# Block-sparse attention and a gated FFN on one core: FFN groups of one chunk in place of two, another order of the attention-value matmuls, and a new order list

## The chip, the cores and the metric

The kernel runs on one core of one Trainium2 chip. Times are device microseconds of that core. The tensor engine is called PE, the vector engine DVE, the scalar engine ACT, GpSimd POOL and the sync engine, which here only issues DMAs, SP.

## The reference, cut to what matters

```python
# q, k, v: (4 batches, 8 heads, 768 tokens, 64); blocks of 32 tokens
scores = np.matmul(q, k.transpose(0, 1, 3, 2)) / np.sqrt(64)
mask   = |block_i - block_j| <= 1, or first/last block row or column, or one of 3 sampled blocks
attn   = softmax(np.where(mask, scores, -1e9))
x      = np.matmul(attn, v)          # heads side by side: (3072 tokens, 512)
gate   = 1 / (1 + np.exp(-(x @ w_gate)))     # 512 -> 1536
val    = x @ w_val
out    = (gate * val) @ w_out                # 1536 -> 512, float32
```

## The kernel before, in words

The work is cut into 12 **chunks** of 256 tokens (three for each batch) and, within a chunk, four **pairs** of heads: 48 pairs, numbered 0 to 47 in the order of the loops over chunk and head pair.

For each pair, `attend` issues three score tiles (`scores`, line 640), each with 256 of the 768 keys against the chunk's 256 queries for both heads. The 64-row matmuls of the two heads use the two halves of the PE array at the same time. ACT takes the exponential of each tile out of PSUM (line 658, tile `pt`), DVE multiplies it by the 0/1 mask (line 666). Then `values` (line 681) forms 24 matmuls of 65 columns into one PSUM bank: 2 query blocks (`jq`) x 2 heads (`hd`) x 6 key blocks (`j`). The 65th column of the values is one, so that it gives the sum of the weights. DVE takes the reciprocal of that sum (line 691) and multiplies (line 695). The result is turned to lie with features on partitions: for the first three chunks by PE (line 720) and a DVE copy (line 725), for the others by a DMA transpose that SP issues (line 708). It is written into a tile `x0` to `x3`.

The FFN (`ffn`) takes the chunks in **groups**. For each of 12 blocks of 128 hidden features, PE forms gate and value projections (line 746), each four matmuls of the group's width; ACT takes tanh of the half gate (line 767, tile `tg`), DVE forms (tanh + 1) x value (line 774, tile `h`). Each **gate step** in the list below is one of the two projections of a block. Output projections (line 791) sum over the 12 blocks for 128 tokens at a time into one bank, in **output steps** of two matmuls; DVE or ACT halves the sum (lines 805, 809) and SP stores it (line 814). In the kernel before, the groups are

```python
GROUPS = [[0], [1], [2], [3, 4], [5, 6], [7, 8], [9, 10], [11]]
```

so that four of them are 512 tokens wide, where a gate matmul has 512 columns and gate and value take a bank each, and four are 256 wide, where both share a bank.

The order of all instructions is made when the program is built. Each step is recorded with an engine, a duration, its inputs and outputs, and a priority (`Plan.op`); `Plan.run` then lays the steps out in time with those durations (an exponential is put at 0.915 us, a value set at 0.79), gives out PSUM banks and ring buffers, and writes each engine's instructions down in the order found. On the chip, each engine runs its own list in order and waits only on semaphores. Where the planner has a choice, it takes the lowest priority number, disturbed by random numbers from `SEED`. From pair `CHAIN` = 28 on, the order of PE's steps is fixed by hand as a chain of **rounds**, one per pair, spelled by

```python
ROUND = "SoVgggoo"
```

in which S is the three score tiles of pair m, V the values of pair m - 1, g about two units of gate steps (a 512-wide step is two units), and o an output step. `WANT` and `READY` hold back outputs and gates until their inputs can be there. `FETCH` says after which pair's scores the later loads of q, k and v are placed, `CAST_LATE` shifts the priority of their casts and transposes. Rings: q, k and v have two staging buffers each, `pt` has 12, each `x` tile has 3.

At the start, PE runs dummy matmuls (line 380) where it would wait, and POOL loads the first batch in half precision, then the FFN weights (lines 521, 531).

Of the kernel before, what the change touches and what calls it, by code (L numbers as in the profile page):

```python
# [9 lines left out]
f16 = mybir.dt.float16  # L10
f32 = mybir.dt.float32
# [7 lines left out]
NJ = S // 128  # L19
NP = H // 2  # L20
NCH = 3
CH = 256
DM = H * D
DFF = 1536
NF = DFF // 128
# [2 lines left out]
VW = 96  # L28
SPIN = 22.0
NMASK = 1  # L30
SEED, MIX = 43, 0.4
WANT, READY = 4, 1
Q0P, M1P, M2P = -39.2, 14, 17
XR, HR, HOLD, HN = 3, 2, 0.4, 1
EARLY = [(0, 0), (1, 0), (0, 1), (0, 2), (0, 3)]
FETCH = ((6, 1), (3, 2))
CHAIN, GLAG, OLAG, ROUND = 28, 9, 16, "SoVgggoo"
EDGES = [0, 768, 1536]
LAND = dict(sbi=1.7, mi=1.6, ident=3.2, e0=3.4, e1=3.3, q=3.1, kb=4.4, k=3.5)
FIRST = [  # L40
# [1 line left out]
]  # L42
HALF = [(0, 0), (0, 1), (0, 2), (0, 3)]
TURN_PE = 3
CAST_LATE = 20
GROUPS = [[0], [1], [2], [3, 4], [5, 6], [7, 8], [9, 10], [11]]
WIDE = CH * max(len(ns) for ns in GROUPS)


class Buf:  # L50
# [220 lines left out]
def kernel(  # L271
# [32 lines left out]

    P = Plan()
    for name, n in (
        ("qs", 2), ("ks", 2), ("vs", 2), ("q16", 4), ("k16", 4), ("qT", 8), ("kT", 8),
        ("v16", 8), ("vh", 4), ("pt", 12), ("rz", 2), ("x16", 4), ("tg", 2), ("y", 3),
    ):
        P.ring(name, n)  # L310
    P.banks(8)
# [284 lines left out]
    def build_mask(c, prio, behind):  # L596
# [21 lines left out]

    group_of = {n: (g, i) for g, ns in enumerate(GROUPS) for i, n in enumerate(ns)}
    xT = {  # L620
        (g, p): sb(f"x{p}", [128, WIDE], f16) for g in range(len(GROUPS)) for p in range(NP)
    }

    valued, scored = {}, []
# [1 line left out]
    def attend(n, p, seq):  # L626
        b, c = divmod(n, NCH)
        masked = n < NMASK
        pts = []
        for tt in range(NCH):  # L630
            st, pt = psb([2, 512], homes=PAIR, span=2), sb("pt", [128, 2, 2, CH], f16)

            def scores(tt=tt, st=st):
                qT, kT = tr["q", b, p](), tr["k", b, p]()
                for jj in range(2):
                    for own in (0, 1) if masked else (1,):
                        for hd in range(2):
                            r = slice(hd * 64, hd * 64 + 64)
                            l, m = (kT, qT) if own else (e24(), bias())
                            nc.tensor.matmul(  # L640
                                st()[:, hd, jj * CH : (jj + 1) * CH],
                                l[r, 2 * tt + jj, :],
                                m[r, 2 * c : 2 * c + 2, :],
                                start=not (own and masked), stop=bool(own),
                            )

            need = [tr["q", b, p], tr["k", b, p]]
            o = P.op(
                "PE", 0.43 if masked else 0.215, scores, reads=[*need, e24, bias] if masked else need,
                writes=[st], prio=seq, mode="row", behind=scored[-1:],  # L650
            )
            if (n, p, tt) == (0, 0, 0):
                o.deps.remove(late)
            scored.append(o)
            o.paired, o.twin = (n, p) not in EARLY and 4 * n + p < CHAIN, psb([2, 512], homes=PAIR, span=2)
            P.op(
                "ACT", 0.915,
                lambda st=st, pt=pt: nc.scalar.activation(  # L658
                    pt().rearrange("p h j q -> p h (j q)"), st(), AF.Exp, scale=SCALE
                ),  # L660
                reads=[st], writes=[pt], prio=seq,
            )

            def masks(tt=tt, pt=pt):
                t = pt().rearrange("p h j q -> p h (j q)")
                nc.vector.tensor_tensor(  # L666
                    t, t, mask()[:, c, tt].unsqueeze(1).to_broadcast([128, 2, 512]), op=ALU.mult
                )

            if not masked:  # L670
                P.op("DVE", 0.61, masks, reads=[pt], writes=[pt], after=[mask_ops[c, tt]], prio=seq)
            pts.append(pt)

        o, rz, x16 = psb([4, 128]), sb("rz", [128, 4, 1], f32), sb("x16", [128, 2, 128], f16)

        def values():
            v_ = v16[b, p]()
            for jq in range(2):
                for hd in range(2):
                    for j in range(NJ):  # L680
                        nc.tensor.matmul(  # L681
                            o()[:, 2 * jq + hd, 0:65],
                            pts[j // 2]()[:, hd, j % 2, jq * 128 : jq * 128 + 128],
                            v_[:, hd, j, 0:65],
                            start=(j == 0), stop=(j == NJ - 1),
                        )

        valued[n, p] = P.op("PE", 0.79, values, reads=[*pts, v16[b, p]], writes=[o], prio=seq + (3.05 if n == 0 and p < 3 else 0.1), mode="full")
        hold = HOLD if n < HN else 0.0
        P.op(  # L690
            "DVE", 0.2, lambda: nc.vector.reciprocal(rz(), o()[:, :, 64:65]), reads=[o], writes=[rz], prio=seq - 5  # L691
        ).hold = hold
        P.op(
            "DVE", 0.36,
            lambda: nc.vector.tensor_tensor(  # L695
                x16().rearrange("p j (h d) -> p (j h) d", d=64),
                o()[:, :, 0:64],
                rz().to_broadcast([128, 4, 64]),
                op=ALU.mult,
            ),  # L700
            reads=[o, rz], writes=[x16], prio=seq - 5,
        ).hold = hold
        g, i = group_of[n]
        dst = xT[g, p]
        if n >= TURN_PE:
            P.op(
                "SP", 1.2,
                lambda: nc.sync.dma_start_transpose(
                    dst()[:, i * CH : (i + 1) * CH].rearrange("p (j q) -> p j q", j=2),
                    x16().rearrange("p j m -> p (j m)"),  # L710
                ),
                reads=[x16], writes=[dst], prio=seq - 5, dma=0.45,
            )
            return
        tT = psb([2, 128], f16)

        def turn():
            dst()
            for jq in range(2):
                nc.tensor.transpose(tT()[:, jq, :], x16()[:, jq, :], ident16())  # L720

        P.op("PE", 0.12, turn, reads=[x16, ident16], writes=[tT, dst], prio=seq - 5, mode="full").hold = hold
        P.op(
            "DVE", 0.28,
            lambda: nc.vector.tensor_copy(
                dst()[:, i * CH : (i + 1) * CH], tT().rearrange("p j q -> p (j q)")
            ),
            reads=[tT], writes=[dst], prio=seq - 5,
        ).hold = hold


    hts, gates, outs, ends = {}, [], [], []

    def ffn(g, seq):
        w = CH * len(GROUPS[g])
# [2 lines left out]
        first = seq - 90 if last else seq  # L738
        for f in range(NF):
            both = psb([512])  # L740
            pair = [(both, 0), (both, 256) if w == 256 else (psb([512]), 0)]
            for k, ((t, z), (nm, wt)) in enumerate(zip(pair, (("g", wg), ("v", wv)))):

                def go(t=t, z=z, wt=wt, f=f):
# [13 lines left out]
                        behind=gates[-1:],  # L758
                    )
                )  # L760
                gates[-1].units, gates[-1].group = w // 256, g
                gates[-1].ready = 4 * GROUPS[g][-1] + 4 + READY
            tg, h_ = sb("tg", [128, WIDE], f32), sb(f"h{f}", [128, WIDE], f16)
            hts[g, f] = h_
            P.op(
                "ACT", 0.17 + 0.43 * k_,
# [12 lines left out]
        for tt in range(w // 128):  # L779
# [4 lines left out]
            for a, z in zip(cuts, cuts[1:]):  # L784
                m, parts = slice(a, z), DM / (z - a)
                py = psb([DM])
                for f0 in range(0, NF, 2):
# [11 lines left out]
                            after=list(w_out.values()), prio=seq + 12 + tt, mode="full", behind=outs[-1:],  # L799
                        )  # L800
                    )
                    outs[-1].wants = min(2 * NF * g + 2 * f0 + WANT, 2 * NF * len(GROUPS))
                P.op(
                    "DVE", 0.69 / parts,
                    lambda py=py, y=y, m=m: nc.vector.tensor_scalar_mul(y()[:, m], py()[:, m], 0.5),
# [8 lines left out]
                    lambda y=y, b=b, j=2 * c + jq, m=m: nc.sync.dma_start(outv[b, j][:, m], y()[:, m]),  # L814
                    reads=[y], prio=0, dma=0.8 / parts,
                )

        ends.append(len(outs))

    seq, turned, late_loads = 0, [], []  # L820
    order = [(n, p) for n in range(B * NCH) for p in range(NP)]
# [27 lines left out]
    for (n, p), o in valued.items():  # L849
        g = group_of[n][0] - XR  # L850
        if g >= 0:
            o.behind.append(gates[2 * NF * (g + 1) - 1])
    chain, gi, oi, room = [], 0, 3 * max(0, CHAIN - OLAG), 6 * (CHAIN - GLAG)
    while room > 0:
        room -= gates[gi].units
        gi += 1
    score = [scored[i : i + NCH] for i in range(0, len(scored), NCH)]
    value = list(valued.values())
    for m in range(CHAIN, len(score) + 12):
        for step in ROUND:  # L860
            if step == "S":
                chain += score[m] if m < len(score) else []
            elif step == "V":
                chain += value[m - 1 : m]
            elif step == "g":
                room = min(room + 2, 2)
                while room > 0 and gi < len(gates) and gates[gi].ready <= m:
                    while gates[gi].group > 1 and oi < ends[gates[gi].group - 2]:
                        chain.append(outs[oi])
                        oi += 1  # L870
                    room -= gates[gi].units
                    chain.append(gates[gi])
                    gi += 1
            elif oi < len(outs) and outs[oi].wants <= gi:
                chain.append(outs[oi])
                oi += 1
    chain += gates[gi:] + outs[oi:]
    for a, z in zip(chain, chain[1:]):
        z.behind.append(a)
    for m, o in late_loads:  # L880
# [32 lines left out]
```

The softmax here doesn't subtract the row's maximum and nothing guards it: scores larger than these inputs give would overflow.

## Time and profile before

| | us |
|---|---|
| median of 5 runs | 290.26 (290.02 to 290.68) |
| the profiled execution's own time | 290.35 |
| its span, from the first to the last instruction | 288.6 |

| engine | busy us | share of the span |
|---|---|---|
| PE | 282.0 | 98% |
| PE weight loads, beside it | 172.3 | 60% |
| ACT | 204.2 | 71% |
| DVE | 186.7 | 65% |
| POOL | 14.8 | 5% |

Busy time of an engine is the union of its instructions. PE's matmuls overlap one another in the pipeline, so the duration of one matmul (379 ns for 512 columns, 273 for 256, 193 for 65) is longer than the distance to the next one; the pieces of the chain of waits, which are laid end to end, show the distance. The granted clock of PE is 0.999 of full speed over the span.

### The profile page before, as it was taken

To read this page: it belongs to the slowest core of one execution; us is meant where nothing else is said; L and a number is where in the kernel's file an instruction comes from. 1 tells how busy PE (TensorE), PEld (TensorE's weight loads), DVE (VectorE), ACT (ScalarE), POOL (GpSimd) and SP (SyncE) were. 2 spreads that over 40 slices of the span, in tenths; PEclk is the share of its full clock that TensorE was granted. 3 is DMA by queue.
4 is the path that set the end of the run, shared out by engine and by line. 5 is a ranking of instruction groups with operands and counts; after the bars stand their busy time and mean duration, and the time that the engine had idled before them with its cause. 6 is when DMAs were issued, how large, how long until landed. Compare 5 with 4: busy or idle time off the path is not lost.

```text
span 288.6 us, 7279 instructions
## 1 busy us (share of the span) xinstructions
PE 282.0 (98%) x3030; PEld 172.3 (60%) x3030; DVE 186.7 (65%) x401; ACT 204.2 (71%) x281; POOL 14.8 (5%) x24
## 2 busy tenths in 40 slices
PE   7898999999999999999999999999999999999995
PEld 6586786687578655555555555554555555447753
DVE  3787997898897876866586576476476474223210
ACT  3869879987898898886888896776776773333321
POOL 8740000000000000000000000000000000000000
PEclk9999999999999999999999999999999999999999
DMA  7999999993698982051869751011011011001013
GB/s 106 170 207 211 208 239 254 242 288 62 219 224 158 256 205 53 18 182 36 218 169 176 218 74 57 24 34 55 13 46 55 11 47 57 37 36 36 10 65 111
DMA packets 50785, 35.25 MB, mean 122 GB/s; under 512 B 31376, under 2 KB 47808, under 8 KB 50752
## 3 DMA queue, kind: packets, MB, share of 16 engines
q1 hardware_dynamic: 43304, 27.71, 37.8%
q0 software_dynamic: 7232, 7.01, 15.2%
q8 instruction: 23, 0.38, 0.5%
q10 hardware_dynamic: 216, 0.07, 0.1%
q14 instruction: 10, 0.08, 0.1%
HBM read 28.42 MB, written 6.29 MB: 120 GB/s over the span
## 4 chain that ended last, share of the span: by engine, by line
PE 93%; DMA 2%; ACT 2%; POOL 2%; issue 0%; ACTq 0%; POOLq 0%
PE psum L746 44%; PE psum L791 23%; PE psum L640 13%; PE psum L681 12%; DMA q<-in_q_dram 2%; ACT pt L658 1%; PE psum L457 1%; PE psum L720 1%; POOL k L439 0%; PE psum L602 0%; POOL k_a L486 0%; POOL k_b L490 0%; POOL q L439 0%; POOL q_late L439 0%; PE psum L380 0%
## 5 line engine op out<-in xcount | busy, mean ns | idle before, releaser
L658 ACT ACTIVATE pt<-psum 128x1024 f16<-128x1024 f32 x144 | 138.9, 1030 | 25.6 <-PE psum L640 25.4
L666 DVE TENSOR_TENSOR pt<-pt,mask 128x1024 f16<-128x1024 f16 x132 | 89.0, 687 | 45.3 <-ACT pt L658 45.2
L746 PE MATMUL psum<-x,wv 128*128 128x256 f16 (+1 forms) x384 | 78.2, 326 | 0.0
L746 PE MATMUL psum<-x,wg 128*128 128x256 f16 (+1 forms) x384 | 78.1, 326 | 0.0
L767 ACT ACTIVATE tg<-psum 128x256 f32<-128x256 f32 (+1 forms) x96 | 47.6, 499 | 41.7 <-PE psum L746 30.6
L791 PE MATMUL psum<-wo,h 128*128 128x512 f16 (+2 forms) x300 | 73.0, 371 | 0.0
L774 DVE SCALAR_TENSOR_TENSOR h<-tg,psum 128x256 f16<-128x256 f32 (+1 forms) x96 | 52.2, 551 | 28.8 <-PE psum L746 15.9
L746 PEld LDWEIGHTS <-wg 128*128 128x128 f16 x384 | 35.9, 98 | 24.3 <-issue 1.7
L746 PEld LDWEIGHTS <-wv 128*128 128x128 f16 x384 | 35.3, 98 | 23.0 <-issue 2.5
L681 PEld LDWEIGHTS <-pt 128*128 128x128 f16 x1152 | 41.0, 97 | 8.8 <-issue 1.1
L640 PE MATMUL psum<-qT,kT 64*128 64x256 f16 x576 | 45.0, 271 | 0.5 <-ACT pt L658 0.4
L791 PEld LDWEIGHTS <-h 128*128 128x128 f16 x300 | 26.3, 98 | 30.2 <-issue 5.7
L681 PE MATMUL psum<-v,pt 128*128 128x65 f16 x1152 | 42.7, 193 | 0.3 <-ACT pt L658 0.3
L640 PEld LDWEIGHTS <-kT 64*128 64x128 f16 x576 | 24.6, 94 | 18.5 <-issue 15.3
L695 DVE TENSOR_TENSOR x<-psum,rz 128x256 f16<-128x256 f32 x48 | 20.4, 424 | 1.7
L809 ACT ACTIVATE y<-psum 128x512 f32<-128x512 f32 (+2 forms) x22 | 12.7, 579 | 11.0 <-PE psum L791 10.8
L691 DVE RECIPROCAL rz<-psum 128x4 f32<-128x4 f32 x48 | 8.6, 179 | 5.1 <-PE psum L681 5.0
L380 PE MATMUL psum<-zero 128*64 128x128 f16 x44 | 5.9, 278 | 1.0 <-DVE zero L350 1.0
L427 ACT CAST q<-qs 128x768 f16<-128x768 f32 x8 | 6.8, 844 | 0.0
L610 DVE TENSOR_SCALAR mask<-psum 128x512 f16<-128x512 f32 x9 | 6.0, 685 | 0.5 <-PE psum L640 0.5
L640 PE MATMUL psum<-bias,e 64*128 64x256 f16 x48 | 6.0, 273 | 0.0
L380 PEld LDWEIGHTS <-zero 128*64 128x64 f16 x44 | 4.3, 147 | 2.1 <-issue 1.1
(54 smaller groups left out, 71.2 us busy)
## 6 DMA issues: line engine op xcount, KB each, us to landing
out_dram<-y SPq DMA_DIRECT2D x23, 256.0 KB, 2.0
qs<-in_q_dram SPq DMA_DIRECT2D x12, 384.0 KB, 4.1
vs<-in_v_dram SPq DMA_DIRECT2D x12, 384.0 KB, 5.0
ks<-in_k_dram SPq DMA_DIRECT2D x12, 384.0 KB, 4.0
wg<-in_moe_w_gate_dram POOLq DMA_DIRECT2D x2, 768.0 KB, 14.0
wv<-in_moe_w_val_dram POOLq DMA_DIRECT2D x2, 768.0 KB, 16.0
wo<-in_moe_w_out_dram POOLq DMA_DIRECT2D x3, 512.0 KB, 21.9
vh<-in_v_dram POOLq DMA_DIRECT2D x4, 192.0 KB, 8.3
```

The costliest lines, as they stand in the source:

```text
L380: "PE", dur, lambda: nc.tensor.matmul(t()[0:64], zero()[:, 0:64], zero(), start=True, stop=True),
L640: nc.tensor.matmul(st()[:, hd, jj * CH : (jj + 1) * CH], l[r, 2 * tt + jj, :], m[r, 2 * c : 2 * c + 2, :], start=not (own and masked), sto ...
L658: lambda st=st, pt=pt: nc.scalar.activation(pt().rearrange("p h j q -> p h (j q)"), st(), AF.Exp, scale=SCALE),
L666: nc.vector.tensor_tensor(t, t, mask()[:, c, tt].unsqueeze(1).to_broadcast([128, 2, 512]), op=ALU.mult)
L681: nc.tensor.matmul(o()[:, 2 * jq + hd, 0:65], pts[j // 2]()[:, hd, j % 2, jq * 128 : jq * 128 + 128], v_[:, hd, j, 0:65], start=(j == 0), ...
L691: "DVE", 0.2, lambda: nc.vector.reciprocal(rz(), o()[:, :, 64:65]), reads=[o], writes=[rz], prio=seq - 5
L695: lambda: nc.vector.tensor_tensor(x16().rearrange("p j (h d) -> p (j h) d", d=64), o()[:, :, 0:64], rz().to_broadcast([128, 4, 64]), op=AL ...
L746: nc.tensor.matmul(t()[:, z : z + w], wt()[:, i, f * 128 : (f + 1) * 128], xT[g, i]()[:, 0:w], start=(i == 0), stop=(i == NP - 1),)
L767: lambda tg=tg, a=pair[0]: nc.scalar.activation(tg()[:, 0:w], a[0]()[:, a[1] : a[1] + w], AF.Tanh, scale=0.5),
L774: lambda tg=tg, a=pair[1], h_=h_: nc.vector.scalar_tensor_tensor(h_()[:, 0:w], tg()[:, 0:w], 1.0, a[0]()[:, a[1] : a[1] + w], op0=ALU.add, ...
L791: nc.tensor.matmul(py()[:, m], hts[g, f]()[:, tt * 128 : (tt + 1) * 128], wo()[:, f, m], start=(f == 0), stop=(f == NF - 1),)
L809: lambda py=py, y=y, m=m: nc.scalar.activation(y()[:, m], py()[:, m], AF.Copy, scale=0.5),
```

## The change

1. `GROUPS` is twelve groups of one chunk. All gate matmuls have 256 columns, gate and value always share a bank. The code for other widths goes, and with it `WANT`, `READY`, `WIDE` and `ends`.
2. The rounds are fixed from pair 16 in place of 28: each has exactly six gate steps, and three output steps from pair 9 on counted by `OLAG`. The first 66 gate steps and 21 output steps are left to the planner.
3. `values` has the key block as its outer loop: the matmuls go over the four slots (2 `jq` x 2 `hd`) of the bank for each key block. Only the first of the 24 carries the start flag. Its planned duration is 0.715 us in place of 0.79.
4. The list is planned anew, with another seed, three staging buffers for q, k and v in place of two, 15 `pt` buffers in place of 12, four of each `x` tile in place of three, and other values of `FETCH` and `CAST_LATE`.

```diff
-SEED, MIX = 43, 0.4
-WANT, READY = 4, 1
+SEED, MIX = 13, 0.4
-XR, HR, HOLD, HN = 3, 2, 0.4, 1
+XR, HR, HOLD, HN = 4, 2, 0.4, 1
-FETCH = ((6, 1), (3, 2))
-CHAIN, GLAG, OLAG, ROUND = 28, 9, 16, "SoVgggoo"
+FETCH = ((6, 1), (1, 2))
+CHAIN, GLAG, OLAG, ROUND = 16, 5, 9, "SoVgggoo"
-CAST_LATE = 20
-GROUPS = [[0], [1], [2], [3, 4], [5, 6], [7, 8], [9, 10], [11]]
-WIDE = CH * max(len(ns) for ns in GROUPS)
+CAST_LATE = 12
+GROUPS = [[i] for i in range(12)]
...
-        ("qs", 2), ("ks", 2), ("vs", 2), ("q16", 4), ("k16", 4), ("qT", 8), ("kT", 8),
-        ("v16", 8), ("vh", 4), ("pt", 12), ("rz", 2), ("x16", 4), ("tg", 2), ("y", 3),
+        ("qs", 3), ("ks", 3), ("vs", 3), ("q16", 4), ("k16", 4), ("qT", 8), ("kT", 8),
+        ("v16", 8), ("vh", 4), ("pt", 15), ("rz", 2), ("x16", 4), ("tg", 2), ("y", 3),
...
         def values():
             v_ = v16[b, p]()
-            for jq in range(2):
-                for hd in range(2):
-                    for j in range(NJ):
+            for j in range(NJ):
+                for jq in range(2):
+                    for hd in range(2):
                         nc.tensor.matmul(
                             o()[:, 2 * jq + hd, 0:65],
                             pts[j // 2]()[:, hd, j % 2, jq * 128 : jq * 128 + 128],
                             v_[:, hd, j, 0:65],
-                            start=(j == 0), stop=(j == NJ - 1),
+                            start=(j + jq + hd == 0), stop=(j == NJ - 1), skip_group_check=True,
                         )
 
-        valued[n, p] = P.op("PE", 0.79, values, reads=[*pts, v16[b, p]], ...
+        valued[n, p] = P.op("PE", 0.715, values, reads=[*pts, v16[b, p]], ...
...
-            pair = [(both, 0), (both, 256) if w == 256 else (psb([512]), 0)]
+            pair = [(both, 0), (both, 256)]
...
-    chain, gi, oi, room = [], 0, 3 * max(0, CHAIN - OLAG), 6 * (CHAIN - GLAG)
-    while room > 0:
-        room -= gates[gi].units
-        gi += 1
+    chain, gi, oi = [], 6 * (CHAIN - GLAG), 3 * max(0, CHAIN - OLAG)
...
-    for m in range(CHAIN, len(score) + 12):
+    for m in range(CHAIN, len(score) + 8):
         for step in ROUND:
             if step == "S":
                 chain += score[m] if m < len(score) else []
             elif step == "V":
                 chain += value[m - 1 : m]
             elif step == "g":
-                room = min(room + 2, 2)
-                while room > 0 and gi < len(gates) and gates[gi].ready <= m:
-                    while gates[gi].group > 1 and oi < ends[gates[gi].group - 2]:
-                        chain.append(outs[oi])
-                        oi += 1
-                    room -= gates[gi].units
-                    chain.append(gates[gi])
-                    gi += 1
-            elif oi < len(outs) and outs[oi].wants <= gi:
-                chain.append(outs[oi])
+                chain += gates[gi : gi + 2]
+                gi += 2
+            elif m >= OLAG:
+                chain += outs[oi : oi + 1]
                 oi += 1
-    chain += gates[gi:] + outs[oi:]
+    chain += outs[oi:]
```

The tiles of the FFN (`x`, `tg`, `h`) are 256 columns wide throughout.

More of the change, by code (lines that the diff above doesn't have):

```diff
@@ L620 @@
     xT = {
-        (g, p): sb(f"x{p}", [128, WIDE], f16) for g in range(len(GROUPS)) for p in range(NP)
+        (g, p): sb(f"x{p}", [128, CH * len(ns)], f16) for g, ns in enumerate(GROUPS) for p in range(NP)
     }
@@ L684, in values @@
                             v_[:, hd, j, 0:65],
-                            start=(j == 0), stop=(j == NJ - 1),
+                            start=(j + jq + hd == 0), stop=(j == NJ - 1), skip_group_check=True,
                         )
-        valued[n, p] = P.op("PE", 0.79, values, reads=[*pts, v16[b, p]], writes=[o], prio=seq + (3.05 if n == 0 and p < 3 else 0.1), mode="full")
+        valued[n, p] = P.op("PE", 0.715, values, reads=[*pts, v16[b, p]], writes=[o], prio=seq + (3.05 if n == 0 and p < 3 else 0.1), mode="full")
         hold = HOLD if n < HN else 0.0
@@ L729, in attend @@
         ).hold = hold
-    hts, gates, outs, ends = {}, [], [], []
+    hts, gates, outs = {}, [], []
     def ffn(g, seq):
@@ L760, in ffn @@
                 )
-                gates[-1].units, gates[-1].group = w // 256, g
-                gates[-1].ready = 4 * GROUPS[g][-1] + 4 + READY
-            tg, h_ = sb("tg", [128, WIDE], f32), sb(f"h{f}", [128, WIDE], f16)
+            tg, h_ = sb("tg", [128, w], f32), sb(f"h{f}", [128, w], f16)
             hts[g, f] = h_
@@ L801, in ffn @@
                     )
-                    outs[-1].wants = min(2 * NF * g + 2 * f0 + WANT, 2 * NF * len(GROUPS))
                 P.op(
@@ L816, in ffn @@
                 )
-        ends.append(len(outs))
     seq, turned, late_loads = 0, [], []
```

## The prediction

> **What bounds the kernel now.** I read the page's chain of waits first, then the stretch table, then the waits of TensorE, and last the end of the chain in order of time.
>
> ```profile
> PE 93%; DMA 2%; ACT 2%; POOL 2%; issue 0%; ACTq 0%; POOLq 0%
> PE psum L746 44%; PE psum L791 23%; PE psum L640 13%; PE psum L681 12%; DMA q<-in_q_dram 2%; ACT pt L658 1%; PE psum L457 1%; PE psum L720 1%; POOL k L439 0%; PE psum L602 0%; POOL k_a L486 0%; POOL k_b L490 0%; POOL q L439 0%; POOL q_late L439 0%; PE psum L380 0%
> ```
>
> 93% of the chain is TensorE (PE): gate and value projections of the FFN (L746), its output projection (L791), scores (L640), attention values (L681). The stretch table says where PE has idle time (columns: stretch, PE, weight loads, DVE, ACT, POOL):
>
> ```profile
> 0.00:14.00 14.00, 11.33 (x160) 8.46 (x160) 8.01 (x29) 8.46 (x10) 11.59 (x20) 1.00 0.98 137
> 14.00:28.00 14.00, 13.18 (x259) 10.00 (x258) 11.11 (x31) 10.67 (x13) 3.21 (x5) 1.00 1.20 208
> 28.00:60.00 32.00, 31.98 (x415) 23.81 (x415) 27.98 (x65) 27.26 (x41) 0.00 (x0) 1.00 1.14 244
> 132.00:241.00 109.00, 109.00 (x1076) 57.96 (x1074) 68.38 (x132) 81.85 (x106) 0.00 (x0) 1.00 0.34 82
> 241.00:288.60 47.60, 44.48 (x287) 25.70 (x283) 11.17 (x22) 13.93 (x29) 0.00 (x0) 0.99 0.15 52
> ```
>
> After 28 us PE is busy without a break until its last matmul at 285.5, and the waits of TensorE hold nothing longer than 1 us; all lie in the first 28 us. ACT is the next fullest, 85% in 28 to 60 us and 75% in the long stretch. So after 28 us the time is the sum of what PE issues. A matmul's own duration is no measure of that, since matmuls overlap; the pieces of the chain are laid end to end and are:
>
> ```profile
> 231.64 2.59 PE psum L746 x12
> 234.23 0.86 PE psum L791 x4
> 235.10 0.76 PE psum L640 x12
> 235.86 0.54 PE psum L791 x2
> 236.39 0.73 PE psum L681 x24
> 237.12 2.59 PE psum L746 x12
> ...
> 268.99 2.62 PE psum L746 x24
> 271.61 1.29 PE psum L791 x6
> 272.91 2.62 PE psum L746 x24
> 275.53 9.97 PE psum L791 x58
> ```
>
> The first six lines are one round per pair of heads, 5.48 us (237.12 - 231.64): gates, outputs, scores, values. Gates 512 wide take 2.59 us for 12 matmuls; the last group, 256 wide, takes 2.62 us for 24. The change turns every one of the first sort into two of the second.
>
> **What the Trainium skill says.** "TensorE: Matmul & The Clock Gate", section "Back-to-back issue gap", prices a warm matmul at N/2.4 + 2.5 ns: 215.8 for 512, 109.2 for 256. The trace agrees (2.59/12 = 216, 2.62/24 = 109). For 65 columns the rule gives 29.6, the trace 0.73/24 = 30.4. The same page, "Step-by-step: what each phase is for", says that the next weights are loaded while a matmul runs; the 256-wide lines above agree, twice the loads for 0.03 us. "PSUM — Partial Sum Buffer", "The four PSUM rules", says that a matmul without the first flag overwrites where the bank's written bit is clear; that is why the new order of values may raise the flag once per bank. It gives no time for it, and no run here shows one.
>
> **The change, part by part.**
>
> *Groups of 256.* Groups 3 to 6 of the old list (two chunks each) are 4 x 12 x 2 x 4 = 384 matmuls of 512 columns, that is 32 pieces of 12. As 32 pieces of 24 they cost 0.03 us more each: +1.0 us (the rounding of 2.59 and 2.62 allows +0.6 to +1.3), all on PE's path. Their 384 more weight loads lie under the matmuls. ACT has 48 tanh of 512 (606 ns) for which come 96 of 256 (393 ns): +8.6 us. DVE has 48 of L774 at 685 ns for which come 96 at 417 ns: +7.1 us. The planner also puts four casts of q, k and v (0.84 on ACT, 0.55 on DVE) from ACT to DVE and two y copies (0.60, 0.69) the other way, which makes ACT +6.4 us in all and DVE +7.9. I cost all of it at nothing, since PE covers them: a round of the new list holds, by these rows, ACT 3 x 1.030 (exponentials) + 3 x 0.393 + half a y copy 0.30 + about 0.3 of casts = 4.9 us, DVE 3 x 0.687 + 0.18 + 0.42 + 3 x 0.417 = 3.9 us plus casts, of PE's 5.51. If that cover were gone, ACT's +6.4 us would show.
>
> *Fixed rounds from pair 16.* Counted in the order of instructions, PE changes between its array modes 131 times before and 131 after (a score visit costs 0.1 us on each side, 0.76 against 12 half-rate matmuls), so this part is nothing. The 32 rounds are those of the long stretch, 2.62 + 1.40 + 0.76 + 0.73 = 5.51. Before pair 16 the list is again the planner's. With the durations above, PE's work ahead of value set 7 is 30.9 us (31.2 before), of set 15 it is 71.3 us (68.5). The trace starts set 15 at 76.1, 7.6 later than its sum, for the waits of the start; the new one should start near 78.9. ACT's work due by then is 64.2 us (63.2), so ACT has 14.6 us to spare in place of 13.0, and DVE 9.7 in place of 7.3. Between set 15 and set 16 stand 22 gate steps, 9.6 us, in which ACT has little to do; nobody waits for that. At the end attention finishes 20 us later, and fewer gates and outputs are left for after it: the same work in another place, and the last output, its y copy and its store are as now.
>
> *Waits.* The third gate pair of a round gives its bank to the next round's values or output, the second gives its to the scores: about 2.0 us of PE work lie between (0.87 + 0.86 + part of a score visit), against 0.39 + 0.42 us for tanh and product. The first gate of a group comes one round after its last values as in the old list: 5.5 us, of which the trace uses 0.7 to 0.9 to issue the transpose (median landing 2.3 us). SP issues the same 24 transposes of q and k, 36 of x and 36 loads; three stage buffers in place of two let loads go out sooner, behind the same weights. I see no queue that gets later.
>
> *Values by key block.* The same 48 x 24 matmuls, with the same operands. What could shorten them is that four sums alternate in the bank, so that one follows itself four matmuls later. The trace speaks against a stall of that kind: by the start times of single matmuls the pitch is 29 ns with every fourth or fifth at 35, while the old order changes sums at every sixth, and two transposes in a row (L720), which sum nothing, show the same 5 ns over the rule. I take 0; the floor by the rule is 29.6, 0.8 x 1152 = -0.9 us; if the fixed 2.5 ns also went, -3.8. Upward I have no reason for more than 1 ns, +1.2 us. The last key block's tile is now first read at the 17th matmul in place of the fifth, 0.36 us later, which helps where values wait for a mask: some 14 places before pair 16, and it is what I set against the shorter leads there (below).
>
> *Start.* The loads, the weights and the first four pairs keep their order; three more filler matmuls (L380) fill waits. I take 0, with -0.5 (the later read, the wait of 0.3 us at L681) to +0.7.
>
> *Sum.* +1.0 on the profiled execution of 290.35 (span 288.6 and 1.75 around it): 291.35. The median of the runs shown is 0.09 under it, so **291.3 us**. A measurement of this kernel tells about 0.2% (0.58 us) from no change.
>
> **Rivals.**
>
> *Late masks in pairs 8 to 15.* The new list gives values 10, 11, 12 and 15 only 2.4 to 2.8 us of PE work after their last scores (old list, same sets: 5.0, 3.3, 5.0, 3.6). An exponential, its mask and two hand-overs need 1.03 + 0.69 + about 0.4 = 2.1, and ACT may be at another tile or a 0.84 cast. The planner prices an exponential at 0.915, the row says 1.030, so ACT runs behind its list. Eight sets late by 0.2 to 0.5 us add 1.6 to 4 us: 293 to 295.3. Against it: the old list has leads of 2.3 to 2.7 at sets 8, 14 and 25 and no wait there. Chance 0.2.
>
> *A shorter value pitch (the other side).* If alternating sums lets a matmul go at 29.6 ns or less, 1152 of them give back 0.9 us and the result is 290.4, no change; from 29.0 ns on the kernel is faster by over 0.2% (1.0 + 0.6 us over 1152 is 1.4 ns), and at 27.1 it stands at 287.5. For it: 0.8 ns per matmul are unexplained by the rule. Against it: the argument above. Chance 0.25, half of it faster.
>
> *ACT rounds overrun.* A round with both a y copy (0.60) and a cast (0.84) holds 5.7 us of ACT, 0.2 over PE's. If each of about 14 such rounds were lost to PE, +2.8: 294. But rounds without them have 0.9 us to spare, so it needs casts in successive rounds. Chance 0.05.
>
> *It does not do what it says.* The narrow gates could cost nothing and the new order of values leave them as they are: 290.3, no change. The first needs the pieces 2.59 and 2.62 to differ by chance; that view has nine of 2.59 and four of 2.62, all alike. It is part of the low end of the forecast.
>
> **How the numbers follow.** The forecast has 0.5, its own range 290.5 to 292.2 (gates 0.6 to 1.3, start -0.5 to +0.7, summed less at once). With the late masks up and the value pitch down, 8 in 10 reach from 289.2 to 294.2; faster than that needs a pitch below 28.6, slower a queue that I did not see. Faster: the lower half of the pitch rival and a luckier start, 0.13. Within 0.2%: the pitch rival's upper half and the low end of the forecast, 0.19. Slower: the rest, 0.68.
>
> **What would show it.** Right: the chain has x24 pieces of 2.62 at the gates and 0.73 at the values from pair 16 to the end, rounds of 5.51, PE at 100% from 28 us on, ACT near 211 us and DVE near 195 us busy in all. Pieces of 0.70 or less at the values show the pitch rival; waits of the value matmuls for DVE masks, or PE under 31.9 of the 32 us from 28 to 60, show the late masks; waits of scores or gates for ACT after 90 us show the overrun. A start of value set 15 far from 78.9 makes my early sum wrong.

## The result, and the profile after

Against the kernel before, measured on the same chips, the changed kernel takes 1.0032 times as long (95% interval 1.0023 to 1.0040): 291.53 us against 290.45, about 0.9 us more by the ratio (0.7 to 1.2). The forecast was 291.3, +1.0.

The chain of waits of the changed kernel by engine and by line, from the page (L744 gates, L787 outputs, L679 values, L638 scores):

```profile
PE 93%; DMA 2%; POOL 2%; ACT 1%; issue 1%; DVE 1%; DVEq 0%; ACTq 0%; POOLq 0%
PE psum L744 44%; PE psum L787 23%; PE psum L679 12%; PE psum L638 12%; DMA q<-in_q_dram 2%; PE psum L718 1%; ACT pt L656 1%; PE psum L455 1%; POOL k L437 0%; DVE x L693 0%; PE psum L600 0%; POOL k_a L484 0%; POOL q L437 0%; POOL q_late L437 0%; POOL k_b L488 0%
```

The same engine with nearly the same shares (scores 12% in place of 13). The stretch table of the changed kernel (stretch, PE, weight loads, DVE, ACT, POOL):

```profile
14.00:28.00 14.00, 13.11 (x263) 10.07 (x262) 10.86 (x31) 10.55 (x13) 2.97 (x4) 1.00 1.19 208
28.00:60.00 32.00, 32.00 (x416) 24.14 (x411) 27.74 (x64) 25.78 (x40) 0.00 (x0) 1.00 1.02 234
132.00:241.00 109.00, 109.00 (x1310) 80.61 (x1309) 74.03 (x166) 84.28 (x133) 0.00 (x0) 1.00 0.36 95
```

PE is full from 28 us on, as before. In the long stretch it issues 1310 matmuls in place of 1076, and its weight loads take 80.6 of the 109 us in place of 58.0, without one gap on PE. The end of the chain in order of time:

```profile
235.06 2.62 PE psum L744 x24
237.68 0.86 PE psum L787 x4
238.55 0.76 PE psum L638 x12
239.31 0.54 PE psum L787 x2
239.85 0.73 PE psum L679 x24
240.58 2.62 PE psum L744 x24
...
277.44 2.62 PE psum L744 x24
280.06 6.09 PE psum L787 x40
```

From the first line to the sixth is one round: 5.52 us (240.58 - 235.06) in place of 5.48. The gates are now 2.62 us in 24 matmuls; nothing else in the round has moved by more than 0.01. At the end 40 output matmuls follow the last gate in place of 58, because more gates were left for later.

### The profile page after: what moved, and what is told of

The parts are those of the page before. It is cut to its first block, busy times and chain, and to the rows that moved or that the text cites. A ratio compares the mean times of both kernels' runs of the same rounds, so it can differ in the third digit from the quotient of the medians.

```text
span 289.0 us, 8130 instructions
## 1 busy us (share of the span) xinstructions
PE 282.8 (98%) x3417; PEld 209.8 (73%) x3417; DVE 193.5 (67%) x451; ACT 209.5 (72%) x327; POOL 14.9 (5%) x24
## 4 chain that ended last, share of the span: by engine, by line
PE 93%; DMA 2%; POOL 2%; ACT 1%; issue 1%; DVE 1%; DVEq 0%; ACTq 0%; POOLq 0%
PE psum L744 44%; PE psum L787 23%; PE psum L679 12%; PE psum L638 12%; DMA q<-in_q_dram 2%; PE psum L718 1%; ACT pt L656 1%; PE psum L455 1%; POOL k L437 0%; DVE x L693 0%; PE psum L600 0%; POOL k_a L484 0%; POOL q L437 0%; POOL q_late L437 0%; POOL k_b L488 0%
## 5 line engine op out<-in xcount | busy, mean ns | idle before, releaser
L744 PE MATMUL psum<-x,wv 128*128 128x256 f16 x576 | 86.4, 273 | 0.0
L744 PE MATMUL psum<-x,wg 128*128 128x256 f16 x576 | 86.3, 272 | 0.0
L763 ACT ACTIVATE tg<-psum 128x256 f32<-128x256 f32 x144 | 56.2, 392 | 38.1 <-PE psum L744 36.5
L770 DVE SCALAR_TENSOR_TENSOR h<-tg,psum 128x256 f16<-128x256 f32 x144 | 57.9, 418 | 26.2 <-ACT tg L763 25.7
L787 PE MATMUL psum<-wo,h 128*128 128x512 f16 (+2 forms) x300 | 75.1, 372 | 0.0
L744 PEld LDWEIGHTS <-wv 128*128 128x128 f16 x576 | 55.9, 98 | 7.2 <-issue 0.8
L744 PEld LDWEIGHTS <-wg 128*128 128x128 f16 x576 | 53.5, 98 | 7.1 <-issue 0.4
L679 PEld LDWEIGHTS <-pt 128*128 128x128 f16 x1152 | 41.0, 98 | 9.9 <-issue 1.2
L638 PE MATMUL psum<-qT,kT 64*128 64x256 f16 x576 | 44.4, 271 | 0.0
L787 PEld LDWEIGHTS <-h 128*128 128x128 f16 x300 | 25.8, 98 | 24.1 <-issue 7.8
L679 PE MATMUL psum<-v,pt 128*128 128x65 f16 x1152 | 42.9, 193 | 0.2 <-ACT pt L656 0.2
L638 PEld LDWEIGHTS <-kT 64*128 64x128 f16 x576 | 24.5, 94 | 18.8 <-issue 15.5
L804 ACT ACTIVATE y<-psum 128x512 f32<-128x512 f32 (+2 forms) x24 | 13.9, 580 | 12.8 <-PE psum L787 12.8
L414 DVE CAST v<-vs 128x768 f16<-128x768 f32 x11 | 6.1, 553 | 0.0
L638 PE MATMUL psum<-bias,e 64*128 64x256 f16 x48 | 6.0, 273 | 0.0
```

The lines of the kernel that those rows point to most:

```text
L638: nc.tensor.matmul(st()[:, hd, jj * CH : (jj + 1) * CH], l[r, 2 * tt + jj, :], m[r, 2 * c : 2 * c + 2, :], start=not (own and masked), sto ...
L679: nc.tensor.matmul(o()[:, 2 * jq + hd, 0:65], pts[j // 2]()[:, hd, j % 2, jq * 128 : jq * 128 + 128], v_[:, hd, j, 0:65], start=(j + jq + ...
L744: nc.tensor.matmul(t()[:, z : z + w], wt()[:, i, f * 128 : (f + 1) * 128], xT[g, i]()[:, 0:w], start=(i == 0), stop=(i == NP - 1),)
L763: lambda tg=tg, a=pair[0]: nc.scalar.activation(tg()[:, 0:w], a[0]()[:, a[1] : a[1] + w], AF.Tanh, scale=0.5),
L770: lambda tg=tg, a=pair[1], h_=h_: nc.vector.scalar_tensor_tensor(h_()[:, 0:w], tg()[:, 0:w], 1.0, a[0]()[:, a[1] : a[1] + w], op0=ALU.add, ...
L787: nc.tensor.matmul(py()[:, m], hts[g, f]()[:, tt * 128 : (tt + 1) * 128], wo()[:, f, m], start=(f == 0), stop=(f == NF - 1),)
```

## The experiments

All are compared with the kernel before. The times of single steps below are read from the start times of single matmuls in the traces. "Values" are given as the time from the first of the 24 matmuls to the next step: 0.729 us in nearly all late rounds of the kernel before, 0.735 in those of the changed kernel.

### Narrow groups alone

```diff
 # the kernel before
-GROUPS = [[0], [1], [2], [3, 4], [5, 6], [7, 8], [9, 10], [11]]
+GROUPS = [[i] for i in range(12)]
```

> The kernel before with groups of one chunk alone; its values, rings and hand-set rounds from pair 28 stay. Issue-sum theory (the time moves by what PE has to issue, and nothing else): 384 gate matmuls of 512 columns become 768 of 256, +1.0 us, and this list has 137 array mode changes in place of 131, +0.6 us: +1.5 us over the kernel before (+0.5%), rounds of 5.51 us in place of 5.48, value sets unchanged at 0.73. Hidden-gain theory (narrow gates cost more, and the new value order gave some of it back in the changed kernel): +2.5 us or more. List theory (the changed kernel's cost is its early list, the narrow gates are free): +0.6 us or less.

Measured: ratio 1.0050 (1.0035 to 1.0065), +1.5 us (1.0 to 1.9). Its chain, one round:

```profile
230.97 2.62 PE psum L746 x24
233.59 0.86 PE psum L791 x4
234.45 0.76 PE psum L640 x12
235.21 0.54 PE psum L791 x2
235.75 0.73 PE psum L681 x24
236.48 2.62 PE psum L746 x24
```

The round is 5.51 us (236.48 - 230.97), values stay at 0.729. The issue sum is met, and both other theories fall: the gates cost neither 2.5 us nor nothing. The two terms can be told apart in its trace. The early list is that of the kernel before, and from the first gate to the last matmul PE takes 258.4 us in place of 256.9, +1.5. A change of array mode costs 96 ns (205 ns from a gate matmul to a score, 109 from one gate matmul to the next), so the six more of them are 0.6 us, and 0.9 is left for the gates.

### The changed kernel with the old order of values

```diff
 # the changed kernel
-            for j in range(NJ):
-                for jq in range(2):
-                    for hd in range(2):
+            for jq in range(2):
+                for hd in range(2):
+                    for j in range(NJ):
...
-start=(j + jq + hd == 0), stop=(j == NJ - 1), skip_group_check=True,
+start=(j == 0), stop=(j == NJ - 1),
```

> The changed kernel with the old order of values (query block, head, key block; a start flag for each sum); the list of all engines is the same. Issue-sum theory: the changed kernel's value sets are 0.735 us apart from the next step against 0.729 before, so 48 of them give back at most 0.3 us: +0.7 us over the kernel before (+0.25%), value sets of 0.729. Hidden-gain theory: without the new value order it is slower than the changed kernel, +2 us or more over the kernel before. If the later first read of the third tile had covered late masks, waits of values for DVE appear between 28 and 80 us, +0.3 to +1 us over the changed kernel.

Measured: ratio 1.0013 (1.0002 to 1.0025), +0.4 us (0.1 to 0.7). Values go back to 0.729 (or 0.730). PE waits for nothing after 28 us, so the later read of the third tile was not needed by this list. The new order is no gain that covers a larger cost: without it the kernel is, if anything, faster. The expected +0.7 lies at the upper end of the interval; why the list costs less than the sum is told under "Sum" below.

### The kernel before with the new order of values

The same edit the other way.

> The kernel before with the new order of values alone; planned durations and so the lists are those of before. Issue-sum theory: value sets go from 0.729 to 0.735 us, +0.1 to +0.3 us in all (0.0 to +0.1%, not to be told from nothing). Hidden-gain theory: -1 us or more. Late-read help (the third tile is first read 0.36 us later): at most -0.3 us, all of it in the one wait for ACT at 25 us.

Measured: ratio 1.0011 (0.9999 to 1.0024), +0.3 us (0.0 to 0.7). Values are at 0.735. This time alone could not be told from nothing; with the trace, 48 x 6 ns = 0.3 us is the size.

### Old order, one start flag

```diff
 # the changed kernel with the old loop order, and still
 start=(j + jq + hd == 0), stop=(j == NJ - 1), skip_group_check=True,
```

Only the first of the 24 matmuls raises the flag; the list is that of the changed kernel.

> The changed kernel with the old loop order of values, but with the start flag on the first of the 24 matmuls alone, as in the new order. If the 6 ns of a value set (0.735 against 0.729) belong to the order in which the matmuls go over slots and tiles: sets of 0.729. If they belong to the flag: sets of 0.735.

Measured: values at 0.729 (one run, 291.22 us). The 6 ns belong to the order, not to the flag. Why that order costs them stays open: the traces show that, among steps of 29 and 30 ns, one of 35 comes six times in 24 matmuls in place of five, not what causes it.

### Values of 96 columns

```diff
 # the changed kernel
-nc.vector.memset(vring[i]()[:, :, :, 64:65], 1.0)
+nc.vector.memset(vring[i]()[:, :, :, 64:VW], 1.0)
-o()[:, 2 * jq + hd, 0:65] ... v_[:, hd, j, 0:65]
+o()[:, 2 * jq + hd, 0:VW] ... v_[:, hd, j, 0:VW]
```

> The changed kernel with value matmuls of 96 columns in place of 65 (the 31 more hold ones and nobody reads them). It measures the 0.8 to 1.0 ns by which the pitch of the values stands over N/2.4 + 2.5. If 65 columns run into a floor on the pair of weight load and matmul near 30.5 ns: at 96 the pitch is 42.5 and even, value sets of 1.02 us. If every fourth or fifth matmul pays 5 to 6 ns whatever its width: 43.7 on average, with single steps of 48, value sets of 1.05 us. Either way +14 to +16 us in all.

Measured: 305.63 us (one run), and in the chain of this kernel:

```profile
230.00 1.02 PE psum L679 x24
231.02 2.62 PE psum L744 x24
```

1.02/24 = 42.5 ns, and from pair 16 on single steps are 42 or 43 without exception. The rule N/2.4 + 2.5 ns that the Trainium skill has in "TensorE: Matmul & The Clock Gate" ("Back-to-back issue gap") gives the same 42.5. The section gives this rule for an isolated matmul; for streams in which every matmul has a weight load it gives about 81 ns at 128 columns and 131 at 512. The runs here do not agree with those two figures: every gate matmul has its own load, and they take 2.68/48 = 55.8 ns at 128 columns (next experiment) and 216 at 512, on the rule. So the 0.8 ns at 65 columns is not a cost on every fourth or fifth matmul whatever its width. The run fits a floor near 30.4 ns on the average of matmuls that come with their own weight loads, which 65 columns (29.6) fall under and 96 do not. It is not shown: the odd width of 65 would fit as well, no other width was tried, and a plain floor would not tell the two orders apart.

### Gates of 128 columns

```diff
 # the changed kernel
-for i in range(NP):
-    nc.tensor.matmul(t()[:, z : z + w], wt()[:, i, f * 128 : (f + 1) * 128], xT[g, i]()[:, 0:w], ...
+for a in range(0, w, 128):
+    for i in range(NP):
+        nc.tensor.matmul(t()[:, z + a : z + a + 128], wt()[:, i, f * 128 : (f + 1) * 128], xT[g, i]()[:, a : a + 128], ...
```

> The changed kernel with each gate matmul of 256 columns cut into two of 128 (one sum after the other, the same weights loaded again), a dose of the suspected cost: 1152 more gate matmuls than the changed kernel, the lists otherwise the same. Issue-sum theory with a fixed cost of about 2.5 ns for each matmul: a gate step goes from 0.437 to 8 x 55.8 = 0.446 us, 288 of them +2.7 us over the changed kernel (+3.6 us, +1.2% over the kernel before), rounds of 5.57 us. Weight-load theory (narrow gates cost because their weights are no longer hidden): at 128 columns a load has half the cover again, steps well over 0.446, +6 us or more over the changed kernel. If the narrow gates' cost were a chance of the lists: no more than +0.5 over the changed kernel.

Measured: ratio 1.0146 (1.0127 to 1.0164), +4.2 us (3.7 to 4.8) over the kernel before, 3.3 over the changed kernel. One round of its chain:

```profile
232.15 2.68 PE psum L745 x48
234.83 0.86 PE psum L788 x4
235.69 0.76 PE psum L638 x12
236.45 0.54 PE psum L788 x2
236.99 0.73 PE psum L679 x24
237.72 2.68 PE psum L745 x48
```

Twelve wide matmuls, 24, and 48 halves take 2.59, 2.62 and 2.68 us: the excess doubles with the number of matmuls, as a fixed cost per matmul does. 48 rounds' worth of gates x 0.06 us = 2.9 of the 3.3. The profiled execution has one new wait besides, of a gate for a transpose of `x` at 268.9 us (0.5 us by the waits of TensorE); why that transpose landed late was not tried. Even at 56 ns a weight load stays hidden; the weight-load theory falls.

### Seed, rings and load places of before

```diff
 # the changed kernel
-SEED, MIX = 13, 0.4
+SEED, MIX = 43, 0.4
-XR, HR, HOLD, HN = 4, 2, 0.4, 1
+XR, HR, HOLD, HN = 3, 2, 0.4, 1
-FETCH = ((6, 1), (1, 2))
+FETCH = ((6, 1), (3, 2))
-CAST_LATE = 12
+CAST_LATE = 20
-        ("qs", 3), ("ks", 3), ("vs", 3), ...
-        ("v16", 8), ("vh", 4), ("pt", 15), ...
+        ("qs", 2), ("ks", 2), ("vs", 2), ...
+        ("v16", 8), ("vh", 4), ("pt", 12), ...
```

> The changed kernel with the seed, the rings and the load places of the kernel before (43; q, k, v 2, pt 12, x 3; FETCH (3, 2), CAST_LATE 20); groups, rounds and values as changed. Its early list is another one, with the same PE work to 0.01 us and 131 mode changes. Issue-sum theory: within 0.3 us of the changed kernel, +0.6 to +1.2 over the kernel before, no PE wait over 0.3 us after 28 us. List theory: the new seed and rings matter, waits of values or gates of 1 us or more between 28 and 90 us, +2 us or more over the kernel before.

Measured: ratio 1.0032 (1.0014 to 1.0049), the same as the changed kernel's. The waits of its TensorE, asked from 28 us on, are this one line (total, times, longest):

```profile
PE psum L638 <- ACT pt L656: 0.4, 1, 0.4
```

Its idle time lies at 27.5 to 27.9 us; the kernel before has the same wait at 27.6 to 28.0. From 28 to 285 us PE is full. Another list, the same sum of work, the same time. Seed, rings and load places brought nothing here, and cost nothing.

### Rounds from pair 16, groups still wide

```diff
 # the kernel before
-CHAIN, GLAG, OLAG, ROUND = 28, 9, 16, "SoVgggoo"
+CHAIN, GLAG, OLAG, ROUND = 16, 5, 9, "SoVgggoo"
```

> The kernel before with its rounds fixed from pair 16 (as in the changed kernel) in place of 28; groups stay two chunks wide, values and rings as before. Its first wide group can't start before round 21, so rounds 17 to 20 hold no gates: 2.9 us of PE work each against ACT's three exponentials and a y copy, about 3.7. Issue-sum theory with the ACT bound: PE's list is 0.4 us shorter in work, but these four rounds are short of PE work, +2 to +3.5 us over the kernel before, all between 90 and 105 us as scores and values waiting for ACT. If fixing rounds early is free by itself (list theory wrong) and the planner's slack covers the four rounds: -0.5 to +0.5 us.

Measured: ratio 1.0294 (1.0270 to 1.0318), +8.5 us. No theory had that size. The waits of its TensorE after 85 us, and PE's busy time in three stretches:

```profile
PE psum L791 <- DVE h L774: 3.6, 6, 0.8
PE psum L746 <- DVE x L695: 1.6, 1, 1.6
...
90.00:105.00 15.00, 13.00 (x192) 1.00 0.81 220
105.00:150.00 45.00, 42.81 (x437) 1.00 0.55 130
150.00:294.00 144.00, 141.27 (x1237) 1.00 0.22 63
```

Between 90 and 105 us PE is idle for 2.0 us, as expected for the four rounds without gates, but most of it is one wait of 1.6 us, and not for ACT. Three lines of the order of time:

```profile
102.29 1.02 PE L681 MATMUL psum<-v,pt 128*128 128x65 f16 x24
...
104.48 0.42 DVE L695 TENSOR_TENSOR x<-psum,rz 128x256 f16<-128x256 f32 x1
...
104.95 1.02 PE L746 MATMUL psum<-x,wg 128*128 128x512 f16 x4 [1.64 <-DVE x L695]
```

The value set is that of pair 20, which is not in the group that this gate takes (pairs 12 to 19). In this kernel's list the gate gets the PSUM bank that the value set just before it has filled, and must wait until DVE has read it. The group's own last `x` landed only 0.2 us earlier, at 104.7, so without the bank the wait would have been about 1.4 us.

The expectation missed the rest, 4.9 us of idle time later: outputs wait for `h` six times. With the gates started late and the outputs started early, an output step stands in the list just behind the gates whose product it sums, as in the lines below, and that goes on to 269 us.

```profile
140.32 1.03 PE L746 MATMUL psum<-x,wv 128*128 128x512 f16 x4
...
141.62 0.69 DVE L774 SCALAR_TENSOR_TENSOR h<-tg,psum 128x512 f16<-128x512 f32 x1
...
142.36 0.82 PE L791 MATMUL psum<-wo,h 128*128 128x512 f16 x3 [0.80 <-DVE h L774]
```

Idle time is less than what the waits cost, since a matmul's own duration outlasts the step to the next: from the first gate to the last matmul PE takes 265.6 us in place of 256.9, +8.7.

The rounds from pair 16 work in the changed kernel because its narrow groups are ready one round after four pairs, not after eight. In its list, by the planned durations, about 3.0 us or more of other PE work stand between an output and the last gate whose product it sums; in the list here five outputs have none.

## Why the prediction was right, point by point

**Gates.** 32 x 0.03 us = +1.0 was taken from pieces that the kernel before already had. (The prediction counts nine pieces of 2.59 in its view of the end; there are eight, and the argument stands.) It holds in the trace (2.62 in every late round), alone (narrow groups, +1.5 with its mode changes) and under a doubled dose. Of the three the dose is the one that tells a fixed cost per matmul from a weight load that is no longer hidden.

**Values.** The forecast took 0 and allowed -3.8 to +1.2. It is +0.3: 0.735 in place of 0.729 in the trace, shown in both directions. The sign is against the hoped gain, and the rival that ended on the other side is refuted. The argument against it was that the steps do not follow the sums, and the traces bear it out: in the old order the 35 ns steps nearly always come at every fifth matmul, while sums change at every sixth. Its second leg does not hold as stated. Of the twelve pairs of transposes (L720) in the kernel before, six have steps of 66 or 67 ns and six of 56, so there is no common 5 ns over the rule (55.8). The argument for the rival, that 0.8 ns stood over the rule, is answered in part: at 96 columns nothing stands over it, and why it does at 65 is open.

**Waits.** No value set waits for a mask after 28 us. The leads of 2.4 to 2.8 us that the late-mask rival pointed at were enough, with the old order of values too. ACT's busy time is 209.5 us (forecast 211), DVE's 193.5 (195), and PE covers both. Set 15 starts at 78.2 us (forecast 78.9).

**Start.** The forecast took 0, with more filler matmuls where PE waits, and that is what the traces show. From the first value matmul to the first gate it is 13.65 to 13.67 us in the kernel before and the three that share its early list (narrow groups, new order of values, rounds from pair 16), and 13.71 to 13.73 in the changed kernel and the three that share its list (old order of values, old order with one flag, gates of 128): +0.1. The matmuls are the same but for three more fillers, which take 0.26 us; the waits from 23 to 28 us sum to 1.0 us in place of 1.3. The first value matmul itself starts anywhere from 14.1 to 15.0 us in these eight executions, early or late with the first loads, and says nothing of the change.

**Sum.** Gates +1.0, values +0.3, start +0.1, and -0.4 that the forecast had at nothing. Half of this is the array mode. The count of 131 changes before and after is right, but the kernel before has 98 of them after its first gate and the changed kernel 96; the other two stand ahead of it, where PE waits in any case. Two at 96 ns are -0.2. The rest, another -0.2, is half one long step of a score at 58.7 us in the profiled execution of the kernel before and half differences of some 10 ns a step. From the first value matmul to the last matmul PE takes 270.6 us before and 271.5 after: +0.9, as measured. That the forecast was so near owes something to luck: it had two terms of opposite sign, +0.3 and -0.4, both at 0.

No run here beats the kernel before. Wider groups would give back 0.03 us for each piece of 12 gate matmuls made from 24: an estimate of less than 0.3 us if two of the four remaining narrow groups were joined, which is below what a measurement tells. A larger sum lies in the changes of array mode: 131 at 96 ns are an estimate of 12.6 us, and no run set out to lower their number.

## What to carry to other kernels

Where one engine is full from end to end, read what it issues from pieces of the chain laid end to end, not from durations, and look for the new shape among those that the old kernel already has: a difference of 0.03 us per piece, counted, was most of the answer. Where things stand counts beside how many there are: of the same 131 mode changes, two moved ahead to where PE waits anyway gave back 0.2 us. Work added to engines that PE covers cost nothing here, so say what covers it and look there afterwards. A hand-set order is tied to the size of what it orders: the same rounds that were free with narrow groups cost 8.5 us with wide ones.

## What the runs showed of the hardware that was not expected

- Matmuls of 65 columns with a weight load each start 30.4 to 30.6 ns apart on average, 0.8 to 1.0 over the rule; with 96 columns it is 42.5, on the rule. What makes the difference was not tried.
- At 65 columns the order over slots and tiles moves the average by 0.25 ns (0.729 and 0.735 us for 24), and the start flag does not.
- A weight load of 128 columns with every matmul leaves no gap on PE at steps of 55.8 ns (gates of 128), nor at 42.5 (values of 96 columns).
